# Routing four chunks of tokens at a time instead of two, in an attention and mixture-of-experts kernel

## The chip, the cores and the metric

The kernel runs on one NeuronCore of a Trainium2 chip. The metric is device time in microseconds (us) of one execution. The engines are named as in the profile: PE is TensorE (matmuls; PEld its weight loads), DVE is VectorE, ACT is ScalarE, POOL is GpSimd, SP is SyncE, which here only issues transfers.

## What is computed

```python
# attention without softmax, B, S, D = 8, 2496, 256, d_qk = 64
scores = matmul(z, z.T) / S
x = u * matmul(maximum(scores, 0) ** 2, v)            # 19968 rows of 256
# mixture of experts over the rows with x @ w_skip > 0, E = 8, F = 1024
logits = x @ w_gate;  e = argmax(logits)              # first of the largest
gate = softmax(logits)[e]
out = x + gate * (maximum(x @ w1[e], 0) @ w2[e])      # other rows: out = x
```

## The kernel before

**Precision.** Matmul operands are split into a high part (rounded to fp32r) and a low part (the rest): `zh, zl`, `vh, vl`, `ah, al`, `hh, hl`. A product is three matmuls: high by high, high by low, low by high. ACT (or DVE) rounds, DVE subtracts.

**Attention stage.** A chunk is 512 columns of queries (the fifth of each batch has 448); there are 8 x 5 = 40 chunks, and each has ten steps `p`, one for each pair of 128-row blocks of keys. `stage(s)` issues the scores of a step (`scores`, 6 matmuls with 64 rows each, into a PSUM tile of tag `"s"`, of which there are two), the ReLU and the square on ACT (lines 376, 377), the rounding to `ah` (386) and the low half `al` on DVE (390). `attend` issues 12 matmuls for each half of D (line 419). Scores run two steps ahead of `attend`. Where a score block was computed for an earlier chunk, its transpose is kept in DRAM (`keep`, DVE line 319) and read back (`recall`). At a chunk's end `finish` evacuates the accumulators (447 on ACT, 449 on DVE), multiplies by u in place (452: the u tile becomes the transposed x, `xT`) and turns it to rows (456) which SP stores.

The order on each engine is that of the program text (`tc.manual_schedule`). Work beside the steps is put off by hand: `todo[s]` holds functions that are called at the end of step `s`, `at(s, f)` counts in half steps, and `later` starts a load and calls its split some steps afterwards.

**Routing.** `routing(cis)` treats the chunks in `cis`, 4 tiles of 128 tokens each; `K = 4 * len(cis)`. Its parts are called at different steps:

- `gates`: 8 matmuls a chunk on PE in the program, 16 in the profile (line 491), with `wgs` as a 128x32 weight in one of four column strips, into a tile `psm` of tag `"s"`
- `logits`: DVE transposes `psm` to `lg` (514; a chunk of 448 columns needs separate transposes and a memset, 517, 518)
- `route`: DVE, six operations (525 to 534): the choice of expert, one-hot in `seq`
- `counts`: DVE, a scan over the tiles (543 to 552), which goes on from `run_cnt`, the count of the routing before
- `gate`: ACT, the exponential (555)
- `place`: four matmuls with 64 rows (564, weights `tri` and `ones`), a copy on ACT (570), seven DVE operations (572 to 579): each token's place in its expert's list
- `put_in(t, t + 2)`: DVE adds an offset (588), POOL puts two tiles' numbers and gates into `lst` in DRAM with two indirect transfers (590)

A routing is made up at the end of chunk 0, 2, 4 ... 38 and takes all chunks since the one before, so two, but one at the first. That of chunk 39 runs in the expert stage with 128-row matmuls.

**Expert stage.** From about 1245 us on, each expert takes units of 256 or up to 512 of its rows: POOL gathers x by `lst` (640), PE turns it (658) and runs the two layers (692, 711), POOL scatters the result (743). `load_w` brings the weights.

**Buffers that the change touches.** `ZBUFS = 7` buffers each for `zh` and `zl`; three u tiles; `rp` holds the routing's small tiles, two buffers of most. `"gap"` and `"gap2"` are tiles that nothing uses. At the start `f0` to `f3` round and split z's tiles 0 and 1 and v's tiles 0 and 1, all before the first scores. [...]

Of the kernel before, what the change touches and what calls it, by code (L numbers as in the profile page):

```python
# [11 lines left out]
I32 = mybir.dt.int32  # L12
# [28 lines left out]

C_REV, C_OFF, C_IDS, C_THR, C_TRI = 0, 64, 128, 132, 152

# [6 lines left out]
def attn_moe(ctx, tc, zT, uT, v, wg, w1, w2, cst, pad, out):  # L50
# [48 lines left out]

    ZBUFS = SZ // QC + 2  # L100

# [63 lines left out]
    def load_u(ci):  # L165
        b, q0, n = chunks[ci]
        uts[ci] = xp.tile([P, 2, QC], F32, name="ut", tag="ut", bufs=3)
        nc.sync.dma_start(uts[ci][:, :, :n], uT[b, :, :, q0 : q0 + n])
# [15 lines left out]
    load_u(0)  # L184
    for f in (f0, f1, f2, f3):
        f()
# [5 lines left out]
    wgs = cpool.tile([P, 2, 32], F32, name="wgs")  # L192
    cpool.tile([P, 88], F32, name="gap")
    nc.scalar.dma_start(wgs, wg)
# [3 lines left out]
    nc.gpsimd.tensor_copy(tri, trif)  # L198
    rev = cs[:, C_REV : C_REV + 64].rearrange("p (t e) -> p t e", e=E)
    eoff = cs[:, C_OFF : C_OFF + 64].rearrange("p (t e) -> p t e", e=E)  # L200
    ids0 = cs[:, C_IDS : C_IDS + 4]
    run_cnt = None
    goes_on = cpool.tile([P, E, 9], BF16, name="goes_on")
    nc.gpsimd.memset(goes_on, 1.0)
# [271 lines left out]
    def routing(cis, rows64=True):  # L476
# [3 lines left out]
        ins = [xTs.pop(ci) for ci in cis]  # L480
        lg = rp.tile([P, 8, 32], F32, name="lg", tag="lg")[:, :K, :]
        psg = []
# [12 lines left out]

        seq = rp.tile([P, E, 9], BF16, name="seq", tag="seq")
        pre = rp.tile([P, E, 9], BF16, name="pre", tag="pre")
        hot = seq[:, :, 1 : K + 1]
        pair = rp.tile([P, 8, 2], I32, name="pair", tag="pair", bufs=3)
        dest = rp.tile([P, 8], I32, name="dest", tag="dest", bufs=3)  # L500

        ex = rp.tile([P, 8, E], F32, name="ex", tag="ex")[:, :K, :]
        sm = rp.tile([P, 8, 1], F32, name="sm", tag="sm")[:, :K, :]

# [15 lines left out]
        def route():  # L520
            mx = rp.tile([P, 8, 1], F32, name="mx", tag="mx")[:, :K, :]
            dl = rp.tile([P, 8, E], F32, name="dl", tag="dl")[:, :K, :]
            rv = rp.tile([P, 8, E], F32, name="rv", tag="rv")[:, :K, :]
            rm = rp.tile([P, 8, 1], F32, name="rm", tag="rm")[:, :K, :]
            nc.vector.tensor_reduce(mx, lg[:, :, 0:E], axis=AX.X, op=ALU.max)
            dls.append(dl)
            nc.vector.tensor_sub(dl, lg[:, :, 0:E], mx.to_broadcast([P, K, E]))

            nc.vector.scalar_tensor_tensor(rv, dl, 0.0, rev[:, :K, :], op0=ALU.is_equal, op1=ALU.mult)
            nc.vector.tensor_reduce(rm, rv, axis=AX.X, op=ALU.max)  # L530
            nc.vector.scalar_tensor_tensor(
                rm, lg[:, :, E : E + 1], 0.0, rm, op0=ALU.is_gt, op1=ALU.mult
            )
            nc.vector.tensor_tensor(
                hot.rearrange("p e t -> p t e"), rev[:, :K, :], rm.to_broadcast([P, K, E]), op=ALU.is_equal
            )

        def counts():
            nonlocal run_cnt
            if run_cnt is None:  # L540
                nc.vector.memset(seq[:, :, :1], 0.0)
            else:
                nc.vector.tensor_copy(seq[:, :, 0], run_cnt)
            if K < 8:
                nc.vector.memset(seq[:, :, K + 1 :], 0.0)
            nc.vector.tensor_tensor_scan(
                *(x.rearrange("p e t -> p (e t)") for x in (pre, goes_on, seq)), 0.0, op0=ALU.mult, op1=ALU.add
            )
            run_cnt = pre[:, :, 8]
            for g, ci in enumerate(cis):  # L550
                b, q0, _ = chunks[ci]
                nc.vector.tensor_scalar_add(pair[:, 4 * g : 4 * g + 4, 0], ids0, float(b * S + q0))
# [4 lines left out]
        def place():  # L557
            ps = spare(rows64)
            ds_ = rp.tile([P, E, 8], F32, name="ds_", tag="ds_")[:, :, :K]
            df = rp.tile([P, 8], F32, name="df", tag="df")[:, :K]  # L560
            halves = list(enumerate(HALF)) if rows64 else [(0, slice(0, P))]
# [6 lines left out]

            c = rp.tile([P, 2, E * 8], F32, name="c", tag="c", bufs=1)[:, : len(halves), : K * E]
            nc.scalar.copy(c, ps[:, : len(halves), : K * E])  # L570
# [43 lines left out]
    idt_e = gp.tile([P, 2 * NFIX, 2], I32, name="idte")  # L614
    gp.tile([P, 32], F32, name="gap2")
    xgs = {"u": [], "f": []}
# [185 lines left out]
    for ci, (b, q0, n) in enumerate(chunks):  # L802
# [14 lines left out]
        if q0 == 0 and b + 1 < B:  # L817

            jobs = [(load_v, 0, 1, 3), (load_z, 0, 1, 6), (load_v, 1, 2, 3), (load_z, 1, 2, 5), (load_v, 2, 2, 7)]
            jobs += [(load_v, 3, 3, 3), (load_v, 4, 3, 4), (load_v, 5, 3, 6), (load_v, 6, 3, 7)]  # L820
            jobs += [(load_v, 7, 4, 2), (load_z, 2, 4, 3), (load_v, 8, 4, 4), (load_z, 3, 4, 5)]
            jobs += [(load_v, 9, 4, 6), (load_z, 4, 4, 7)]
            for load, j, c, k in jobs:
                later(s0 + c * NB + 2 * k - 7, 7, load, b + 1, j, nc.vector)
# [25 lines left out]
    for s in range(LA):  # L850
        for f in stage(s):
            f()
    accs = {}
    new, left = [], []
    for s, (ci, p) in enumerate(steps):
# [20 lines left out]
        else:  # L876
# [30 lines left out]
            if ci < NC - 1:  # L907
                after = [(rows0, 2), (rows1, 3), (store, 4), (store, 8)]
                if ci % 2 == 0:
                    gates, logits, route, counts, gate, place, put_in = routing(new)  # L910
                    after = [(gates, 2), (logits, 2), (rows0, 2), (rows1, 3), (route, 4), (counts, 4),
                             (store, 5 if ci == NC - 2 else 4), (gate, 5), (place, 6), (store, 8)]
                    for t in range(0, 4 * len(new), 2):
                        f = lambda put_in=put_in, t=t: put_in(t, t + 2)
                        if s + 6 + t < len(steps):
                            after.append((f, 6 + t))
                        else:
                            left.append(f)
# [22 lines left out]
    def end_counts():  # L941
# [11 lines left out]

        late = rp.tile([P, 8, 1], F32, name="late", tag="sm")[:, 0, :]
        nc.vector.tensor_scalar(
# [18 lines left out]
    def turned(e, i):  # L974
        if e and i == 0:
            if not xtf:
                for _ in range(2):
                    t = xp.tile([P, 2 * QC], F32R, name="xtf", tag="ut", bufs=3)
                    xtf.append(t[:, 80 : 80 + QC].rearrange("p (d q) -> p d q", d=2))
            return xtf  # L980
# [147 lines left out]
```

## Time and profile before

| | us |
|---|---|
| median of three runs | 1725.46 |
| lowest, highest | 1724.9, 1727.47 |
| the profiled execution | 1724.65 |
| its span, first to last instruction | 1722.7 |

The granted clock of TensorE was 0.999 of full speed over the span. In the rows below times are in us from the span's start, unless they are marked ns or stand as a mean; a row of a timeline has start, length, engine, line, operation, what is written and read, and how many instructions were merged into it (`x4`). A bracket at its end tells how long the engine had been idle, and who ended that. A length of a matmul is modelled and longer than the time to the next one's start.

### The profile page before, as it was taken

The numbers are of one execution on the slowest core, as the hardware profiler recorded it, in microseconds if no ns is written. First come the engines' busy times: TensorE is split into PE (matmuls) and PEld (weight loads), VectorE is DVE, ScalarE is ACT, GpSimd is POOL, SyncE is SP. The second block draws the span as 40 slices with busy tenths as digits, with TensorE's granted clock in tenths as the row PEclk, the third lists the DMA queues.
The fourth block names the chain that finished last, engine by engine and source line by source line (L and its number), as shares of the span: only waits on it lengthen the run. The fifth ranks groups of instructions, "written<-read, shape, count | busy, mean of one in ns | idle before, by whom it ended". The sixth has DMA issues, their size and how long they took to land.

```text
span 1722.7 us, 39254 instructions
## 1 busy us (share of the span) xinstructions
PE 1710.2 (99%) x15474; PEld 1522.8 (88%) x15474; DVE 1199.4 (70%) x1969; ACT 1118.9 (65%) x1416; POOL 519.6 (30%) x516
## 2 busy tenths in 40 slices
PE   9999999999999999999999999999999999999998
PEld 7888889988888898888889988888999999999997
DVE  7877877887887888778888778777754334344433
ACT  8877877787687778768777886877433333333321
POOL 1103203212311320231132132122355556645731
PEclk9999999999999999999999999999999999999999
DMA  5586699589868958985895799578752333323210
GB/s 191 144 212 188 154 248 285 144 209 263 246 148 235 260 165 203 273 265 135 226 250 178 197 259 276 134 216 223 212 130 76 88 95 107 91 63 97 87 43 27
DMA packets 408108, 303.25 MB, mean 176 GB/s; under 512 B 202768, under 2 KB 346001, under 8 KB 407152
## 3 DMA queue, kind: packets, MB, share of 16 engines
q1 hardware_dynamic: 393728, 276.37, 59.0%
q0 software_dynamic: 13632, 22.99, 4.7%
q8 instruction: 137, 2.24, 0.5%
q14 instruction: 179, 1.47, 0.3%
q10 hardware_dynamic: 432, 0.18, 0.0%
HBM read 184.21 MB, written 136.02 MB: 186 GB/s over the span
## 4 chain that ended last, share of the span: by engine, by line
PE 93%; DMA 3%; issue 2%; ACT 1%; DVE 1%; POOL 0%; SPq 0%; POOLq 0%; ACTq 0%; DVEq 0%
PE acc L419 59%; PE y L711 12%; PE psh L692 11%; PE ps L302 9%; DMA out<-o,idt 2%; PE psm L491 1%; PE pst L658 1%; PE ps L285 0%; DMA out<-xr 0%; DVE al L390 0%; DMA raw<-in_v 0%; ACT r L377 0%; ACT ah L386 0%; ACT r L376 0%; DVE rt L319 0%
## 5 line engine op out<-in xcount | busy, mean ns | idle before, releaser
L419 PE MATMUL acc<-ah,vh 64*128 64x512 f32 (+1 forms) x3120 | 639.6, 383 | 0.8 <-DVE ah L386 0.8
L419 PE MATMUL acc<-ah,vl 64*128 64x512 f32 (+1 forms) x3120 | 625.5, 382 | 0.0
L390 DVE TENSOR_TENSOR al<-r,ah 128x1024 fp32r<-128x1024 f32 (+1 forms) x400 | 479.0, 1205 | 134.7 <-ACT ah L386 128.3
L419 PE MATMUL acc<-al,vh 64*128 64x512 f32 (+1 forms) x3120 | 496.4, 383 | 0.4 <-DVE al L390 0.2
L590 POOL DMA_INDIRECT lst<-pair,dest x160 | 202.0, 1262 | 765.9 <-DVE dest L588 735.8
L386 ACT CAST ah<-r 128x1024 fp32r<-128x1024 f32 (+1 forms) x363 | 370.0, 1030 | 82.3 <-PE acc L419 46.9
L419 PEld LDWEIGHTS acc<-ah,vh 64*128 64x128 f32 x3120 | 325.8, 184 | 49.3 <-issue 1.4
L419 PEld LDWEIGHTS acc<-ah,vl 64*128 64x128 f32 x3120 | 326.0, 184 | 43.6 <-DVE vl L122 0.3
L419 PEld LDWEIGHTS acc<-al,vh 64*128 64x128 f32 x3120 | 309.8, 184 | 51.0 <-DVE al L390 6.3
L376 ACT ACTIVATE r<-ps 128x1024 f32<-128x1024 f32 (+1 forms) x224 | 227.9, 1018 | 132.5 <-PE ps L302 123.8
L697 ACT ACTIVATE hh<-psh 128x512 fp32r<-128x512 f32 (+2 forms) x172 | 96.4, 571 | 269.4 <-PE psh L692 254.2
L377 ACT ACTIVATE r<-r 128x1024 f32<-128x1024 f32 (+1 forms) x224 | 235.9, 1053 | 7.1
L711 PE MATMUL y<-w2t,hh 128*128 128x256 f32 (+1 forms) x1328 | 235.2, 280 | 0.0
L698 DVE SCALAR_TENSOR_TENSOR hl<-psh,hh 128x512 fp32r<-128x512 f32 (+2 forms) x172 | 110.2, 655 | 138.6 <-ACT hh L697 131.5
L319 DVE STREAM_TRANSPOSE rt<-r 128x512 f32<-128x512 f32 x304 | 197.4, 687 | 9.4 <-DMA kept<-rt 8.6
L711 PEld LDWEIGHTS y<-w2t,hh 128*128 128x128 f32 (+1 forms) x1328 | 200.6, 185 | 1.2
L711 PE MATMUL y<-w2t,hl 128*128 128x256 f32 (+1 forms) x664 | 184.2, 277 | 0.0
L692 PE MATMUL psh<-xt,w1h 128*128 128x256 f32 (+3 forms) x896 | 181.1, 300 | 1.9 <-DVE hl L698 1.9
L692 PEld LDWEIGHTS psh<-xt,w1h 128*128 128x128 f32 x896 | 140.4, 188 | 7.2 <-DVE hl L698 3.2
L692 PE MATMUL psh<-xt,w1l 128*128 128x256 f32 (+3 forms) x448 | 133.8, 299 | 0.0
L743 POOL DMA_INDIRECT out<-o,idt x77 | 76.4, 992 | 159.3 <-DVE o L740 126.4
L711 PEld LDWEIGHTS y<-w2t,hl 128*128 128x128 f32 (+1 forms) x664 | 122.6, 185 | 0.0
(197 smaller groups left out, 1735.4 us busy)
## 6 DMA issues: line engine op xcount, KB each, us to landing
kept<-rt SPq DMA_DIRECT2D x242, 256.0 KB, 4.9
r<-kept SPq DMA_DIRECT2D x90, 512.0 KB, 6.0
r<-kept SPq DMA_DIRECT2D x62, 448.0 KB, 7.2
raw<-in_v SPq DMA_DIRECT2D x80, 256.0 KB, 5.8
ut<-in_uT SPq DMA_DIRECT2D x32, 512.0 KB, 6.2
xr<-xrow SPq DMA_DIRECT2D x128, 128.0 KB, 3.7
out<-xr SPq DMA_DIRECT2D x32, 512.0 KB, 6.4
raw<-in_w SPq DMA_DIRECT2D x64, 256.0 KB, 4.0
```

The costliest lines, as they stand in the source:

```text
L302: nc.tensor.matmul(to, k[h, o : o + P], queries(ci, q, h, n), start=(m == 0), stop=(m == 2))
L319: nc.vector.transpose(t[:, :, 32 * k : 32 * k + 32].rearrange("p (k a) i -> p a k i", k=4), r[:, x, :].rearrange("p (a k i) -> p a k i", a ...
L376: nc.scalar.activation(r[:, :, :n], ps[:, :, :n], AF.Relu, scale=isc)
L377: nc.scalar.activation(r[:, :, :n], r[:, :, :n], AF.Square)
L386: (nc.scalar.copy if on_act(ci, p) else nc.vector.tensor_copy)(h_, r_)
L390: nc.vector.tensor_sub(l_, r_, f32(h_))
L419: nc.tensor.matmul(acc[t][:, :n], w[h, x, dd], a[h, x, :n], start=(first and t not in halves[:m]), stop=(last and t not in halves[m + 1 :]),)
L590: put = nc.gpsimd.indirect_dma_start(out=lst, out_offset=bass.IndirectOffsetOnAxis(ap=dest[:, t : t + 1], axis=0), in_=pair[:, t, :], in_o ...
L692: nc.tensor.matmul(ps[:, j * W : (j + 1) * W], wt[:, a, o : o + P], x[:, d, :W], start=(m == 0), stop=(m == 5),)
L697: nc.scalar.activation(hh[:, : G * W], ps[:, : G * W], AF.Relu)
L698: nc.vector.scalar_tensor_tensor(hl[:, : G * W], ps[:, : G * W], 0.0, f32(hh[:, : G * W]), op0=ALU.max, op1=ALU.subtract)
L711: nc.tensor.matmul(ys[t], h[:, tt], w2t[f][:, k, :], start=(f == 0 and m == 0 and t % share == 0), stop=(f == NF - 1 and m == 2), skip_gro ...
```

## The change

1. A routing is made up after chunks 0, 4, 8 ... 36 and after 38 (of the last two). Tiles for up to `KG = 16` token tiles; to find the room most of them have one buffer, and `c` shares a buffer with `lg`. With four chunks `counts` is called at step 5 behind the chunk's end (4 before), `place` at 7 (6), and the eight pairs of puts at 7, 8, 10, 11, 13, 14, 16, 17 (four at 6, 8, 10, 12).
2. Five u tiles in place of three, `ZBUFS` 6 in place of 7; the load of z's tile 1 for batch 1 moves from chunk 2 to chunk 4 of batch 0.
3. `f3`, the split of v's tile 1, is called after the first step's `stage`.
4. The scratch for indirect transfers is 8192 bytes.

```diff
+KG = 16
-C_REV, C_OFF, C_IDS, C_THR, C_TRI = 0, 64, 128, 132, 152
+C_REV, C_OFF, C_IDS, C_THR, C_TRI = 0, 128, 256, 260, 280
-    ZBUFS = SZ // QC + 2
+    ZBUFS = SZ // QC + 1
-        uts[ci] = xp.tile([P, 2, QC], F32, name="ut", tag="ut", bufs=3)
+        uts[ci] = xp.tile([P, 2, QC], F32, name="ut", tag="ut", bufs=5)
-    for f in (f0, f1, f2, f3):
+    for f in (f0, f1, f2):
         f()
-    cpool.tile([P, 88], F32, name="gap")
+    cpool.tile([P, 440], F32, name="gap")
-        lg = rp.tile([P, 8, 32], F32, name="lg", tag="lg")[:, :K, :]
+        lg = rp.tile([P, KG, 32], F32, name="lg", tag="lg", bufs=1)[:, :K, :]
...
-            c = rp.tile([P, 2, E * 8], F32, name="c", tag="c", bufs=1)[:, : len(halves), : K * E]
+            c = rp.tile([P, 2, E * KG], F32, name="c", tag="lg", bufs=1)[:, : len(halves), : K * E]
-    gp.tile([P, 32], F32, name="gap2")
+    gp.tile([P, 408], F32, name="gap2")
-            jobs = [(load_v, 0, 1, 3), (load_z, 0, 1, 6), (load_v, 1, 2, 3), (load_z, 1, 2, 5), (load_v, 2, 2, 7)]
+            jobs = [(load_v, 0, 1, 3), (load_z, 0, 1, 6), (load_v, 1, 2, 3), (load_v, 2, 2, 7)]
+            jobs += [(load_z, 1, 2, 5) if b else (load_z, 1, 4, 6)]
     for s in range(LA):
         for f in stage(s):
             f()
+        if s == 0:
+            f3()
-                if ci % 2 == 0:
+                if ci % 4 == 0 or ci == NC - 2:
                     gates, logits, route, counts, gate, place, put_in = routing(new)
-                    after = [(gates, 2), (logits, 2), (rows0, 2), (rows1, 3), (route, 4), (counts, 4),
-                             (store, 5 if ci == NC - 2 else 4), (gate, 5), (place, 6), (store, 8)]
+                    many = len(new) > 2
+                    after = [(gates, 2), (logits, 2), (rows0, 2), (rows1, 3), (route, 4), (counts, 5 if many else 4),
+                             (store, 5 if ci == NC - 2 else 4), (gate, 5), (place, 7 if many else 6), (store, 8)]
                     for t in range(0, 4 * len(new), 2):
                         f = lambda put_in=put_in, t=t: put_in(t, t + 2)
-                        if s + 6 + t < len(steps):
-                            after.append((f, 6 + t))
+                        k = 6 + (1 + 3 * t // 4 if many else t)
+                        if s + k < len(steps):
+                            after.append((f, k))
-    nc = bacc.Bacc("TRN2", target_bir_lowering=False, num_devices=1)
+    nc = bacc.Bacc("TRN2", target_bir_lowering=False, num_devices=1, dynamic_dma_scratch_size=8192)
```

The other lines of the diff write `KG` for 8, `KG + 1` for 9 and `KG * E` for 64 in the routing's tiles and constants.

## Rows read from the trace of the kernel before

**Rows 1.** The profile's page: busy time of the engines (share of the span, instructions), and the shares of the chain of work that ended last, by engine.

```profile
PE 1710.2 (99%) x15474; PEld 1522.8 (88%) x15474; DVE 1199.4 (70%) x1969; ACT 1118.9 (65%) x1416; POOL 519.6 (30%) x516
PE 93%; DMA 3%; issue 2%; ACT 1%; DVE 1%; POOL 0%; SPq 0%; POOLq 0%; ACTq 0%; DVEq 0%
```

**Rows 2.** The waits of PE's matmuls, first and last of five rows: engine and line that waited, for whom; us in total, times, longest.

```profile
PE psh L692 <- DVE hl L698: 1.9, 3, 1.1
...
PE acc L419 <- DVE al L390: 0.2, 1, 0.2
```

**Rows 3.** The longest wait of PE's weight loads, same columns.

```profile
PEld acc L419 <- DVE al L390: 6.3, 18, 0.6
```

**Rows 4.** One piece of the chain in order of time, in undisturbed attention: start, us, what, how many.

```profile
118.46 5.45 PE acc L419 x48
```

**Rows 5.** PE's timeline around the gates of two chunks.

```profile
174.86 0.61 PE L419 MATMUL acc<-al,vh 64*128 64x512 f32 x4
175.40 1.07 PE L491 MATMUL psm<-ut,wgs 128*32 128x128 f32 x32
176.41 0.50 PE L302 MATMUL ps<-zqh,zh 64*128 64x512 f32 x2
176.75 0.40 PE L302 MATMUL ps<-zql,zh 64*128 64x512 f32 x2
```

**Rows 6.** PE's timeline around the gates of one chunk (chunk 0).

```profile
50.24 0.61 PE L419 MATMUL acc<-al,vh 64*128 64x512 f32 x4
50.78 0.65 PE L491 MATMUL psm<-ut,wgs 128*32 128x128 f32 x16
...
51.70 0.40 PE L302 MATMUL ps<-zql,zh 64*128 64x512 f32 x2
```

**Rows 7.** PE's timeline around the placing of one chunk (first two rows) and of two chunks.

```profile
64.68 0.61 PE L419 MATMUL acc<-al,vh 64*128 64x512 f32 x4
...
65.51 0.39 PE L302 MATMUL ps<-zql,zh 64*128 64x512 f32 x2
...
129.42 0.61 PE L419 MATMUL acc<-al,vh 64*128 64x512 f32 x4
129.88 0.21 PE L564 MATMUL psm<-seq,tri 64*128 64x64 bf16 x2
...
130.26 0.39 PE L419 MATMUL acc<-ah,vl 64*128 64x512 f32 x2
```

**Rows 8.** The instructions that write or read `psm`, over the whole span: duration in ns (least, median, most), first and last start, forms.

```profile
L570 ACT COPY c<-psm x21: 185/257/265, 65.7 to 1252.7; 128x128 f32<-128x128 f32 x19, 128x64 f32<-128x64 f32 x1, 128x32 f32<-128x32 f32 x1
```

**Rows 9.** The start: rows of ACT's timeline, and PE's first two groups of `al` matmuls.

```profile
6.73 0.62 ACT L121 CAST vh<-raw 128x512 fp32r<-128x512 f32 x1
7.26 1.02 ACT L376 ACTIVATE r<-ps 128x1024 f32<-128x1024 f32 x1
9.27 1.00 ACT L376 ACTIVATE r<-ps 128x1024 f32<-128x1024 f32 x1
11.41 0.73 PE L419 MATMUL acc<-al,vh 64*128 64x512 f32 x4
13.61 0.62 PE L419 MATMUL acc<-al,vh 64*128 64x512 f32 x4
```

**Rows 10.** The one-hot, DVE's longest routing operation, by shape, with 64 elements (two chunks) and 32 (one chunk): busy us, mean ns of one, idle time before.

```profile
L534 DVE TENSOR_TENSOR seq<-cs,rm 128x64 bf16<-128x64 f32 x19 | 8.6, 452 | 0.6
L534 DVE TENSOR_TENSOR seq<-cs,rm 128x32 bf16<-128x32 f32 x2 | 0.6, 304 | 0.1
```

**Rows 11.** DVE's timeline in chunk 7: first and last of `route` (6 rows), last of `counts` (4 rows), first of `place` and the first put's (8 rows).

```profile
251.15 0.18 DVE L525 TENSOR_REDUCE mx<-lg 128x8 f32<-128x64 f32 x1
...
252.34 0.45 DVE L534 TENSOR_TENSOR seq<-cs,rm 128x64 bf16<-128x64 f32 x1
...
253.41 0.17 DVE L552 TENSOR_SCALAR pair<-cs 128x4 int32<-128x4 f32 x1 [0.20 <-issue]
...
257.62 0.18 DVE L572 TENSOR_REDUCE sm<-ex 128x8 f32<-128x64 f32 x1
...
259.26 0.17 DVE L588 TENSOR_SCALAR dest<-df 128x2 int32<-128x2 f32 x1
```

**Rows 12.** The transposes behind the gates of rows 5 (DVE's timeline, first and last), and the scores that next use their PSUM buffer (PE's).

```profile
178.79 0.47 DVE L514 STREAM_TRANSPOSE lg<-psm 128x128 f32<-128x128 f32 x2
179.43 0.26 DVE L518 STREAM_TRANSPOSE lg<-psm 32x64 f32<-32x64 f32 x1
179.94 0.39 PE L302 MATMUL ps<-zqh,zh 64*128 64x512 f32 x2
```

**Rows 13.** POOL's longest wait; an indirect gather behind another; and the indirect transfers of the expert stage and the puts by line, with the median us from issue to landing.

```profile
POOL lst L590 <- DVE dest L588: 735.8, 65, 52.8
1268.08 1.00 POOL L640 DMA_INDIRECT xgu<-xr,go  x1 [0.30 <-DVE o L740]
lst<-pair,dest POOLq DMA_INDIRECT x160, 5.9
out<-o,idt POOLq DMA_INDIRECT x77, 2.8
xgf<-xr,go POOLq DMA_INDIRECT x48, 3.3
xgu<-xr,go POOLq DMA_INDIRECT x48, 2.9
```

More of the change, by code (lines that the diff above doesn't have):

```diff
@@ L198, in attn_moe @@
     nc.gpsimd.tensor_copy(tri, trif)
-    rev = cs[:, C_REV : C_REV + 64].rearrange("p (t e) -> p t e", e=E)
-    eoff = cs[:, C_OFF : C_OFF + 64].rearrange("p (t e) -> p t e", e=E)
+    rev = cs[:, C_REV : C_REV + KG * E].rearrange("p (t e) -> p t e", e=E)
+    eoff = cs[:, C_OFF : C_OFF + KG * E].rearrange("p (t e) -> p t e", e=E)
     ids0 = cs[:, C_IDS : C_IDS + 4]
     run_cnt = None
-    goes_on = cpool.tile([P, E, 9], BF16, name="goes_on")
+    goes_on = cpool.tile([P, E, KG + 1], BF16, name="goes_on")
     nc.gpsimd.memset(goes_on, 1.0)
@@ L494, in gates @@
                         )
-        seq = rp.tile([P, E, 9], BF16, name="seq", tag="seq")
-        pre = rp.tile([P, E, 9], BF16, name="pre", tag="pre")
+        seq = rp.tile([P, E, KG + 1], BF16, name="seq", tag="seq")
+        pre = rp.tile([P, E, KG + 1], BF16, name="pre", tag="pre")
         hot = seq[:, :, 1 : K + 1]
[L499 to L503, printed above, removed]
+        pair = rp.tile([P, KG, 2], I32, name="pair", tag="pair", bufs=3)
+        dest = rp.tile([P, KG], I32, name="dest", tag="dest", bufs=3)
+        ex = rp.tile([P, KG, E], F32, name="ex", tag="ex", bufs=1)[:, :K, :]
+        sm = rp.tile([P, KG, 1], F32, name="sm", tag="sm")[:, :K, :]
         def logits():
@@ L520, in route @@
         def route():
[L521 to L524, printed above, removed]
+            mx = rp.tile([P, KG, 1], F32, name="mx", tag="mx")[:, :K, :]
+            dl = rp.tile([P, KG, E], F32, name="dl", tag="dl", bufs=1)[:, :K, :]
+            rv = rp.tile([P, KG, E], F32, name="rv", tag="rv", bufs=1)[:, :K, :]
+            rm = rp.tile([P, KG, 1], F32, name="rm", tag="rm")[:, :K, :]
             nc.vector.tensor_reduce(mx, lg[:, :, 0:E], axis=AX.X, op=ALU.max)
@@ L543, in counts @@
                 nc.vector.tensor_copy(seq[:, :, 0], run_cnt)
-            if K < 8:
+            if K < KG:
                 nc.vector.memset(seq[:, :, K + 1 :], 0.0)
@@ L548, in counts @@
             )
-            run_cnt = pre[:, :, 8]
+            run_cnt = pre[:, :, KG]
             for g, ci in enumerate(cis):
@@ L558, in place @@
             ps = spare(rows64)
-            ds_ = rp.tile([P, E, 8], F32, name="ds_", tag="ds_")[:, :, :K]
-            df = rp.tile([P, 8], F32, name="df", tag="df")[:, :K]
+            ds_ = rp.tile([P, E, KG], F32, name="ds_", tag="ds_", bufs=1)[:, :, :K]
+            df = rp.tile([P, KG], F32, name="df", tag="df")[:, :K]
             halves = list(enumerate(HALF)) if rows64 else [(0, slice(0, P))]
@@ L952, in end_counts @@
         nc.vector.tensor_reduce(nmore, more, axis=AX.X, op=ALU.add)
-        late = rp.tile([P, 8, 1], F32, name="late", tag="sm")[:, 0, :]
+        late = rp.tile([P, KG, 1], F32, name="late", tag="sm")[:, 0, :]
         nc.vector.tensor_scalar(
@@ L977, in turned @@
                 for _ in range(2):
-                    t = xp.tile([P, 2 * QC], F32R, name="xtf", tag="ut", bufs=3)
+                    t = xp.tile([P, 2 * QC], F32R, name="xtf", tag="ut", bufs=5)
                     xtf.append(t[:, 80 : 80 + QC].rearrange("p (d q) -> p d q", d=2))
@@ L1104 @@
     cst[:, C_TRI : C_TRI + P] = np.triu(np.ones((P, P)), 1)
-    cst[:, C_REV : C_REV + 64] = np.tile(E - np.arange(E), 8)
-    cst[:, C_OFF : C_OFF + 64] = np.tile(np.arange(E) * CAP - BIG, 8)
+    cst[:, C_REV : C_REV + KG * E] = np.tile(E - np.arange(E), KG)
+    cst[:, C_OFF : C_OFF + KG * E] = np.tile(np.arange(E) * CAP - BIG, KG)
     tok = np.arange(4 * P).reshape(4, 4, 32).transpose(0, 2, 1).reshape(P, 4)
```

## The prediction

> **What bounds the kernel now.** I read the page first [rows 1]: the multiplying engine (PE) is busy for 1710.2 of 1722.7 us and is 93% of the chain that ended last. The list of waits [rows 2] says the same from the other side: PE's matmuls stood idle for a named engine in five kinds of wait, from 1.9 us down to 0.2 us, so 9.5 us at the very most. Its weight loads waited for the vector engine's (DVE's) low halves 18 times, 6.3 us, at most 0.6 us at once [rows 3]. So until about 1245 us the time is the length of PE's own queue, and a change there gains what it takes out of that queue. It gains nothing by making DVE, ACT or POOL lighter.
>
> The busy digits can't show what the queue loses between two kinds of matmul, because a matmul's modelled length (0.39 us for a pair) is longer than its pitch. The timeline's starts show it. The undisturbed pitch is 48 matmuls in 5.45 us [rows 4], 0.227 us for a pair that runs in the two 64-row halves.
>
> **The gates.** In [rows 5] a block of 32 gate matmuls (two chunks) stands between attention pairs. The four `al` matmuls before it start at 174.86; two pairs later, at 175.31, the next thing could start, and a second pair after it at 175.54. With the block in between, the second pair starts at 176.75: the block costs 1.21 us. In [rows 6] the block of one chunk has 16 matmuls: three pairs on from 50.24 is 50.92, the second pair starts at 51.70, cost 0.78 us. So 16 matmuls more cost 0.43 us, and what is left, 0.78 - 0.43 = 0.35 us, is paid per block whatever is in it. It is seen as 0.09 us before the first gate matmul and 0.34 instead of 0.23 us between the first two pairs behind it; the rest is the end of the block.
>
> Placing does the same on a smaller scale [rows 7]: 129.42 + 0.68 = 130.10, second pair at 130.26, 0.16 us with 64 columns for each matmul; with 32 columns, 64.68 + 0.68 = 65.36 against 65.51, 0.15 us.
>
> **How many blocks go.** There are 40 chunks. Before, a routing closes after chunks 0, 2, 4 ... 38, and one for the last chunk runs in the expert stage: 21, which the 21 copies of `c` confirm (19 with 8 tiles, 2 with 4) [rows 8]. After, it closes after chunk 0, after 4, 8 ... 36 (nine of four chunks), after 38 (two chunks), and the last: 12. Nine blocks of each kind go. The number of gate matmuls (640) stays.
>
> - Gates: 9 x 0.35 = 3.15 us. Reading a start to 0.01 us at three places leaves 2.8 to 3.4.
> - Placing: before, 19 x 0.16 + 0.15 = 3.2 us. After, 0.15 + 0.16 + 9 blocks with 128 columns, a form that the trace does not show. From below it costs what 64 columns cost, 0.16. From above, its two pairs of 128 columns each take as long as a whole 512-column pair does for a quarter of its columns (0.057) on top of a block: 0.16 + 0.11 = 0.27. With 32 columns it was 0.15, so doubling them cost 0.01; from 64 to 128 the columns should begin to count, and I take 0.22, the middle. That is 2.3, a saving of 0.9 us (0.5 to 1.45).
>
> **The start.** `f3` rounds and splits v's second tile before the first activation. In [rows 9] ACT's copy starts at 6.73 and the first ReLU follows it at 7.26. With `f3` behind step 0 the ReLU takes the copy's place, so the first `ah` and `al`, and PE's first `al` matmul at 11.41, come 0.53 us earlier, up to 0.7 if the copy itself had waited for its tile. But the copy now stands before the ReLU of step 1, which then stays near 9.27, and the split stands on DVE between the first `al` and the second `ah`. PE meets its next condition at 13.61, the second `al`, which follows step 1's ReLU and so can come hardly sooner than before; what PE gains there is what it had waited behind other matmuls. Bounds are 0 and 0.7; I take 0.25 us.
>
> **What is moved and hidden.** DVE's small operations become fewer and longer. From 32 to 64 elements the choice's costliest grows by half, 0.304 to 0.452 us [rows 10]. If from 64 to 128 all grew by half, `route` (251.15 to 252.8, 1.65 us) [rows 11] would be 2.5 us; it is a burst of 2.5 us now with `counts` (to 253.6), which goes to the next step, so neither burst exceeds the old one. `place`, now one step later, is 1.8 us (257.62 to 259.4); its bounds are 1.8 and 2.7, and I take 2.2, since its operations are the short ones. All this is hidden while PE's step (30 matmuls with scores, 3.4 us by the pitch in [rows 4], 24 without, 2.7) is longer than DVE's work; if it isn't, the next `al` is late (first rival). The logits of four chunks are up to six transposes in place of four, which hold a score buffer longer. In [rows 12] they run 178.79 to 179.69 and that buffer's next scores start at 179.94, a margin of 0.25 us. After, PE comes 0.86 us later (32 more gate matmuls) and DVE ends 0.47 us later (two transposes more at 0.235, the pitch there): margin 0.64 us, no wait. [...]
>
> The 16 indirect puts go to steps 7 to 17 in pairs; POOL stood idle 735.8 us before puts [rows 13], and the chunk's `straight` copies stand ahead of the puts of their step. The u tiles' fourth and fifth buffers keep four chunks' x until their gates; the slot that a load takes is that of five chunks before, whose gates ran a half chunk earlier, so SP's loads wait for nothing new. One z buffer fewer moves one z load of batch 1 to chunk 4 of batch 0, where it adds a copy on ACT (0.62 us for such a tile in [rows 9]) and a split on DVE: nothing to the path while the step has room, some 0.6 us once if it has none.
>
> **Sum.** 3.15 + 0.9 + 0.25 = 4.3 us off. The profiled execution took 1724.65 (span 1722.7), so 1720.35; the median of the runs, 1725.46, is 0.8 above it and would come to 1721.15. I forecast 1720.7, between the two. About 0.2%, 3.45 us, is what a measurement here can tell from no change; from the median that is 1722.0.
>
> **Rivals.**
> 1. *DVE gives it back.* Place: `place` one step nearer the chunk's end, where DVE also evacuates accumulators. [Rows 11] show the risk: from 251.15 to 259.4 DVE pauses once, for 0.20 us. Price: 0.4 us longer plus the 0.1 us that PE loses when it restarts (0.34 instead of 0.23 us behind the gates in [rows 5]), in nine routings: 4.5 us. With the 4.3 gained that is 1725.6, no change. For it: the full stretch. Against: nine other bursts vanish, and all 21 and everything else cost at most 6.3 us together [rows 3]. Half of it, 1723, is no change too. Chance 0.25.
> 2. *The saving is swallowed later*, at the chunk ends where `al` is late anyway: then only blocks far from one count, say half, 2.2 us, 1723.2. Against: PE has next to no idle time to swallow it. Chance 0.07.
> 3. *Slower: the halved scratch.* Each indirect transfer of the expert stage is issued 1.3 us after the one before and lands about 3 us after its issue [rows 13], so two or three are under way. If the halved scratch holds only one, POOL waits out each landing: the stage's 173 gathers and stores would take 173 x 3 = 519 us in a stage of 478 (from 1245 to the end), and x for the matmuls would come late: some 40 us and more, 1765. It decides once fewer than three fit. Nothing in the trace says how many the old size held beyond what was under way, some four puts (5.9 us to land, two of them a step). Chance 0.04. [...]
> Small delays of several kinds that together exceed 8 us: 0.04, also slower.
>
> **Numbers.** Forecast 0.60 for a gain of about 4.3 us; its own range, with the terms' bounds and runs that differ by 2.5 us, is 1718.5 to 1722. Faster by over 0.2%: 0.60. Within: rivals 1 and 2, 0.32. Slower: 0.08. For 8 in 10 the range goes from 1718 up to the end of rival 1: 1718 to 1726.
>
> **What would show it.** Twelve copies of `c`; blocks of 64 gate matmuls that cost about 2.07 us by the reading above, and placing blocks near 0.22. PE's first `al` matmul near 10.9 instead of 11.41, with a wait before the second. The row of weight loads waiting for `al` at or under 6.3 us: if it is over 10, rival 1 holds. If POOL's indirect rows are longer than 1.3 us apart where they stand back to back, rival 3 holds. The forecast is wrong if the fixed 0.35 us grows with the block, or if moved tiles change the pitch of 0.227 us.

## The result and the profile after

On one chip the changed kernel took 1738.6 us against 1726.8 us (medians): ratio 1.0064, 95% interval 1.0049 to 1.0078. These are its fast runs; a sixth, slow one took 8890 us and is not counted. It is 11.8 us slower, where 4.3 us faster was forecast, and lies outside the range of 1718 to 1726. The profiled execution took 1738.62 us (span 1736.5) against 1724.65 (span 1722.7).

| us | attention ends (start of PE's last `acc` matmul) | from there to PE's last matmul | from there to the end |
|---|---|---|---|
| before | 1242.5 | 473.3 | 7.0 |
| after | 1247.1 | 480.1 | 9.3 |

Between the two profiled executions the loss has three places: +4.6 us in attention, where the gain of 4.3 was due, +6.8 in the expert stage, whose program is unchanged, and +2.3 behind PE's last matmul. Lines of after are one higher than before's from the start to the middle of the program.

The page (busy; shares of the chain) answers [rows 1]: PE's share falls from 93 to 81%, and DMA's rises from 3 to 7%.

```profile
PE 1714.8 (99%) x15438; PEld 1531.7 (88%) x15438; DVE 1183.0 (68%) x1840; ACT 1117.3 (64%) x1398; POOL 518.8 (30%) x516
PE 81%; DMA 7%; DVE 3%; issue 3%; ACT 2%; POOL 1%; SPq 1%; POOLq 0%; DVEq 0%; ACTq 0%
```

The waits of PE's weight loads answer [rows 3] (waiter, for whom: us in total, times, longest). `al` is late 34 times instead of 18, and `ah`, which ACT rounds, is late 8 times.

```profile
PEld acc L420 <- DVE al L391: 13.4, 34, 0.7
PEld acc L420 <- ACT ah L387: 5.8, 8, 2.2
```

PE's timeline, first at the start and then around the first gates of four chunks, answers [rows 9] and [rows 5].

```profile
10.83 0.73 PE L420 MATMUL acc<-al,vh 64*128 64x512 f32 x4
...
13.35 0.73 PE L420 MATMUL acc<-al,vh 64*128 64x512 f32 x4
...
173.21 0.61 PE L420 MATMUL acc<-al,vh 64*128 64x512 f32 x4
173.76 1.95 PE L492 MATMUL psm<-ut,wgs 128*32 128x128 f32 x64
175.63 0.50 PE L303 MATMUL ps<-zqh,zh 64*128 64x512 f32 x2
175.97 0.40 PE L303 MATMUL ps<-zql,zh 64*128 64x512 f32 x2
...
192.31 0.61 PE L420 MATMUL acc<-al,vh 64*128 64x512 f32 x4
...
193.19 0.39 PE L303 MATMUL ps<-zql,zh 64*128 64x512 f32 x2
```

The first `al` matmul is at 10.83 (10.9 forecast). The block of 64 gate matmuls costs 175.97 - 173.21 - 0.68 = 2.08 us (2.07 forecast), placing with 128 columns 193.19 - 192.31 - 0.68 = 0.20 (0.22 forecast). `c` is copied 12 times. So the gain is there, as computed; other things take it away. Three are seen at once in the profile.

**Late scores.** The chain of waits between 229 and 239 us, where PE loses 1.9 us, and what PE then waits for:

```profile
229.22 7.30 DMA r<-kept
...
236.62 1.05 ACT ah L387
237.71 0.51 PE L420 MATMUL acc<-ah,vh 64*128 64x512 f32 x2 [1.76 <-ACT ah L387]
```

The same recall in the kernel before, SP's issue and the `ah` that follows its landing:

```profile
228.31 1.44 SPq L359 DMA_DIRECT2D r<-kept  x1
234.61 1.05 ACT L386 CAST ah<-r 128x1024 fp32r<-128x1024 f32 x1 [0.58 <-DMA r<-kept]
```

Recalled scores land 7.3 us after their issue, and `ah` starts only then. In before the issue is 0.9 us sooner and `ah` starts 6.3 us behind it, not 7.4. Sixteen puts run from 197 to 231 us, in before eight from 197 to 216. At 850 us, twenty chunks on, the same happens (a recall that lands 7.6 us after its issue).

**The last branch.** PE's timeline at the last expert's branch, and the windows behind it (length, PE, PEld, DVE, ACT, POOL busy, granted clock, DMA share, GB/s; in brackets instructions). The last two rows of the first list are the kernel before's:

```profile
1627.16 0.60 PE L659 MATMUL pst<-ident,xgf 128*128 128x128 f32 x4
1630.17 0.66 PE L693 MATMUL psh<-xt,w1h 128*128 128x256 f32 x2 [2.42 <-issue]
1620.03 0.60 PE L658 MATMUL pst<-ident,xgf 128*128 128x128 f32 x4
1620.38 0.48 PE L692 MATMUL psh<-xt,w1h 128*128 128x256 f32 x2
```

```profile
1627.00:1630.20 3.20, 0.79 (x8) 0.58 (x6) 1.48 (x3) 0.58 (x1) 3.04 (x5) 1.00 0.35 72
1630.20:1634.00 3.80, 3.80 (x19) 3.80 (x20) 0.15 (x1) 0.60 (x1) 2.88 (x4) 0.55 0.32 82
1634.00:1639.00 5.00, 5.00 (x45) 5.00 (x44) 2.61 (x5) 2.27 (x4) 0.79 (x1) 1.00 0.15 54
```

PE waits for nothing that the profile shows ("issue"): 3.0 us from one row to the next, 0.35 in before. Behind the pause the granted clock is 0.55 on the mean of the stretch, and 19 matmuls run in its 3.8 us where the later rate (45 in 5.00 us) gives 34; the 15 missing cost 1.7 us. Together 4.4 us.

**The end.** From the start of POOL's last transfer to the end of the span it is 1736.5 - 1728.33 = 8.2 us, in before 1722.7 - 1716.82 = 5.9.

### The profile page after: what moved, and what is told of

Same layout as the page of the kernel before. It is cut to its first block, busy times and chain, and to the rows that moved or that the text cites. A ratio compares the mean times of both kernels' runs of the same rounds, so it can differ in the third digit from the quotient of the medians.

```text
span 1736.5 us, 39038 instructions
## 1 busy us (share of the span) xinstructions
PE 1714.8 (99%) x15438; PEld 1531.7 (88%) x15438; DVE 1183.0 (68%) x1840; ACT 1117.3 (64%) x1398; POOL 518.8 (30%) x516
## 4 chain that ended last, share of the span: by engine, by line
PE 81%; DMA 7%; DVE 3%; issue 3%; ACT 2%; POOL 1%; SPq 1%; POOLq 0%; DVEq 0%; ACTq 0%
PE acc L420 52%; PE y L712 10%; PE psh L693 9%; PE ps L303 8%; DMA r<-kept 3%; DMA out<-o,idt 2%; DVE al L391 2%; DMA xgf<-xr,go 1%; PE psm L492 1%; ACT ah L387 1%; PE pst L659 1%; ACT r L377 1%; ACT r L378 1%; SPq L470 0%; PE ps L286 0%
## 5 line engine op out<-in xcount | busy, mean ns | idle before, releaser
L420 PE MATMUL acc<-ah,vh 64*128 64x512 f32 (+1 forms) x3120 | 648.3, 383 | 3.6 <-ACT ah L387 3.3
L420 PE MATMUL acc<-ah,vl 64*128 64x512 f32 (+1 forms) x3120 | 635.4, 382 | 0.0
L420 PE MATMUL acc<-al,vh 64*128 64x512 f32 (+1 forms) x3120 | 505.2, 384 | 1.3 <-DVE al L391 0.5
L420 PEld LDWEIGHTS acc<-ah,vh 64*128 64x128 f32 x3120 | 338.1, 184 | 51.8 <-ACT ah L387 5.8
L420 PEld LDWEIGHTS acc<-ah,vl 64*128 64x128 f32 x3120 | 337.8, 184 | 41.7 <-DVE vl L123 0.3
L420 PEld LDWEIGHTS acc<-al,vh 64*128 64x128 f32 x3120 | 315.7, 184 | 55.0 <-DVE al L391 13.4
L264 POOL CAST zqh<-zh 128x512 fp32r<-128x512 f32 (+2 forms) x47 | 36.6, 790 | 494.1 <-PE ps L286 209.2
```

The lines of the kernel that those rows point to most:

```text
L420: nc.tensor.matmul(acc[t][:, :n], w[h, x, dd], a[h, x, :n], start=(first and t not in halves[:m]), stop=(last and t not in halves[m + 1 :]),)
```

## The experiments

The experiments ran on several chips; on some the kernel before took 1726 to 1727 us and on others 1736 to 1737, so ratios are to its runs beside them. "Pause" is that of the last branch, from PE's transposes of `xgf` to the next matmul; "end" is from the start of POOL's last transfer (the expectations count it from that transfer's end, 1.0 us less). The ratios come from all counted runs, the other three columns from one profiled execution each, so differences of a microsecond or two between rows of different chips say little. One chip ran `x0_after`, `e7_sparse`, `e5_early` and `e6_noputs`; one `e1_two` to `e4_dense`; one `x1_before`, `e9_light`, `e10_b12k` and `e11_bnoputs`; one the other six.

| kernel | ratio to before (95%) | attention ends | pause | end |
|---|---|---|---|---|
| before, twice (`x1_before`) | | 1242.5, 1242.9 | 0.35, 0.35 | 5.9, 5.8 |
| after | 1.0064 (1.0049 to 1.0078) | 1247.1 | 3.0 | 8.2 |
| `x0_after` | 1.0064 (1.0046 to 1.0082) | 1251.9 | 3.0 | 8.2 |
| `e1_two` | 1.0018 (1.0004 to 1.0031) | 1242.7 | 0.35 | 7.9 |
| `e2_scratch` | 1.0016 (1.0004 to 1.0027) | 1243.5 | 0.35 | 8.0 |
| `e3_f3` | 0.9993 (0.9981 to 1.0004) | 1243.0 | 0.35 | 5.8 |
| `e4_dense` | 1.0336 (1.0294 to 1.0378) | 1294.2 | 3.7 | 8.0 |
| `e7_sparse` | 1.0072 (1.0046 to 1.0098) | 1245.0 | 3.2 | 8.0 |
| `e5_early` | 1.0066 (1.0048 to 1.0084) | 1247.8 | 3.1 | 7.9 |
| `e6_noputs` | not compared | 1242.3 | 3.2 | |
| `e11_bnoputs` | not compared | 1244.3 | 0.35 | |
| `e15_pace` | 1.0056 (1.0038 to 1.0073) | 1243.1 | 3.4 | 7.9 |
| `e9_light` | 1.0024 (1.0013 to 1.0034) | 1240.5 | 3.2 | 7.9 |
| `e12_pad` | 1.0047 (1.0029 to 1.0065) | 1244.9 | 0.35 | 8.1 |
| `e14_bpad` | one run | 1244.1 | 2.4 | 5.8 |
| `e10_b12k` | 1.0004 (0.9992 to 1.0016) | 1243.5 | 0.35 | 6.3 |
| `e13_all` | 1.0079 (1.0058 to 1.0100) | 1246.6 | 0.35 | 5.8 |
| `e16_apart` | 1.0019 (1.0002 to 1.0035) | 1241.8 | 0.35 | 8.0 |
| `e17_room` | 1.0022 (1.0004 to 1.0039) | 1244.9 | 0.35 | 6.0 |

### Which part of the change

```diff
# e1_two (to after)
-                if ci % 4 == 0 or ci == NC - 2:
+                if ci % 2 == 0 or ci == NC - 2:
# e2_scratch (to before)
-num_devices=1)
+num_devices=1, dynamic_dma_scratch_size=8192)
# e3_f3 (to before): only f3 moved, as in the change
```

> The changed kernel with its routing made up after every second chunk, as before, with the old steps for counts, place and puts; the tiles, the five u tiles, the six z buffers, the moved z load, f3 behind the first step and the halved scratch stay as changed. It tells the size of a routing apart from the memory around it. Theory P (the puts and the longer routing are late and lie beside transfers of the chunk after next): the 12 us of loss are gone and the time is that of before, 1726, less 0.3 for the start. Theory D (DVE's bursts, one step later): the same, 1726; P and D are told apart by other runs. Theory M (the halved scratch, the fewer z buffers or moved addresses): the loss stays, 1736 or more, since the gain of fewer blocks (4 us) is given up and nothing of the loss is. Theory C (the expert stage and the end lose time by where the program's instructions lie, or by chance): about 1731, with the end of attention near 1242 as before and about 5 us lost behind it.

> The kernel before with the halved scratch for indirect transfers alone. Theory M says slower by several us, in the expert stage above all, where the changed kernel lost about 7 us behind the end of attention (at most 1733). Theories P, D and C say no change: 1726, with attention's end near 1242.5 and the expert stage as long as before, 480 us.

> The kernel before with f3, the split of v's second tile, called behind the first step's stage and nothing else. In the trace of the changed kernel PE's lag behind the kernel before was -0.26 us after the start. All theories: 0.26 us less than before (1726.5), which a time can hardly show; the profile's first al matmul and the start of the second step should show it. If the rest of the program shifts by more than 1 us in either direction, something in it hangs on the phase of the start.

Routing two chunks with all the rest of the change ends attention where before did and has no pause. So both go with the routing of four, and the z and u buffers and moved loads cost nothing that shows there. The scratch alone (8192 bytes in place of before's 16384) costs as much as all of `e1_two`, some 3 us by the ratios, of which 2.1 are at the end. `f3` alone can't be told from no change.

### The puts

```diff
# e4_dense (to after): k = 7, 7, 8, 8, 9, 9, 10, 10
-                        k = 6 + (1 + 3 * t // 4 if many else t)
+                        k = 6 + (1 + t // 4 if many else t)
# e7_sparse: k = 7, 11, ... 35;  e15_pace: k = 7, 9, ... 21 (both up to chunk 32's routing)
+                        k = 6 + (1 + (2 * t if ci < NC - 4 else 3 * t // 4) if many else t)
+                        k = 6 + (1 + (t if ci < NC - 4 else 3 * t // 4) if many else t)
# e5_early: counts at 4, place at 6, as before
# e6_noputs, e11_bnoputs: in put_in
+                if K == KG:                             # e6_noputs, to after
+                    continue
+                if K == 8 and cis[-1] < NC - 4:         # e11_bnoputs, to before
+                    continue
```

> The changed kernel with its puts drawn together: four at each of the steps 7 to 10 behind a routing's close, so that they end inside the next chunk, in place of two at each of the steps 7, 8, 10, 11, 13, 14, 16, 17. Theory P: the losses that were seen beside late puts (236, 850 us: 2 us each; 573 and 1187, 1.3 us each) go, and the end of attention comes 4 us or more sooner than the 1247.1 of the changed kernel, 1243 or less; if bunched puts only move the crowding, new stalls appear inside the next chunk. Theory D: no change at the end of attention, 1247 (DVE's place and counts stand where they were). Theory M: no change.

I had taken a long run of puts for the harm, and closer puts for a remedy. The kernel is 62 us slower than the one before, and attention 47 us longer than in the changed kernel. The waits of PE's weight loads, and the windows around one run of puts (445 to 470 us):

```profile
PEld acc L420 <- issue: 41.9, 66, 1.4
```

```profile
450.00:455.00 5.00, 5.00 (x50) 4.31 (x46) 3.19 (x6) 2.69 (x4) 3.99 (x4) 1.00 0.94 308
455.00:460.00 5.00, 4.67 (x37) 3.11 (x33) 3.06 (x5) 1.11 (x2) 3.88 (x4) 1.00 0.94 248
460.00:465.00 5.00, 3.96 (x24) 2.25 (x25) 2.12 (x3) 2.32 (x3) 3.97 (x4) 1.00 0.93 158
465.00:470.00 5.00, 3.76 (x14) 1.70 (x13) 1.91 (x3) 0.08 (x1) 3.89 (x4) 0.73 1.03 256
470.00:475.00 5.00, 4.32 (x21) 3.99 (x23) 2.20 (x3) 2.82 (x4) 1.55 (x3) 0.50 0.72 157
```

PE slows from 50 matmuls in 5 us to 14, and then the clock falls too, to 0.73 and 0.50. It waits for nothing that the profile shows; that it starves for its own instructions is the reading that I take, and not shown. The trace has packets of 16384 bytes on an instruction queue of their own (`q8`, 136 in the changed kernel), which I take for PE's; between 444 and 480 us they come 16.9 and 19.3 us apart. That alone proves nothing: in before two come 18.1 us apart (437.72, 455.79) while PE stays busy.

> The changed kernel once more, beside the three others of this call, since the kernel before has moved from 1726 to 1736 us between the first comparison and the second. All theories: its ratio to the kernel before stays near 1.0064, with attention's end near 1247 and the rest of the loss in the expert stage. If the loss behind attention is chance or the place of the program's instructions, the expert stage is now no longer than that of the other kernels.

> The changed kernel with its pairs of puts thinned out: one pair every fourth step (7, 11, 15 ... 35 behind the close) for the routings of chunks 4 to 32, in place of eight pairs within eleven steps. [...] Theory P: attention ends near 1239 to 1241 (before 1242.5, changed 1247.1), the predicted 4 us are there, and the time is some 6 us under the changed kernel. Theory D (place and counts are late on DVE): attention still ends near 1247.

> The changed kernel with counts at step 4 and place at step 6 behind the close, as before, and the puts where the change has them. Theory D: the waits for al (13.4 us on PE's weight loads) fall towards 6 and attention ends 3 us or more sooner than 1247. Theory P: no change there, or worse, since route and counts then stand in one burst: 1247 to 1249.

> The changed kernel without the indirect puts of its nine routings of four chunks; their tokens' numbers are missing from the lists, so the experts gather padding rows for them and only the attention stage is to be read. Theory P: attention ends at the predicted place or sooner, 1238 us, and the recalled scores (r from kept) land on time at 236 and 850 us. Theory D: the stalls at 236, 573, 850 and 1187 us stay and attention ends near 1247.

`x0_after` repeats the ratio and the pause, but attention ends 4.8 us later than in the first profile of the same kernel, and its expert stage, 485.0 us, is about as long as that of `e1_two` (484.5) and `e2_scratch` (485.9), on another chip of the slower kind. So the 6.8 us that the expert stage lost in the first pair of profiles are not seen there.

Thinner puts end attention 6.9 us sooner than `x0_after` on the same chip, and no puts 9.5 us. In `e7_sparse` 2.4 us of what is left are one place (596 us), where a pair of puts stands ahead of the `zqh` copies on POOL. Its time didn't follow: its four runs differed by 9 us, and the profiled one was the quickest. The row of `al` waits in `e6_noputs` is 11.4 us, so DVE's part stays without puts. `e5_early` is a miss for DVE as I had put it: the waits stay at 11.4 us, against 12.3 in `x0_after`. Its attention ends 4.1 us sooner than `x0_after`'s, but gains this at 239, 482 and 851 us, where `e6_noputs` gains too.

On this chip a part of the puts' price is again waits of PE's weight loads for nothing that is seen, in attention 6.6 us in `x0_after` and 1.2 in `e6_noputs` (0.6 in the first profile of the changed kernel):

```profile
PEld acc L420 <- issue: 6.6, 13, 1.2
PEld acc L420 <- issue: 1.2, 6, 0.2
```

What else the puts do is seen in one window, 220 to 235 us, of `x0_after`, then `e6_noputs` (same chip), then `x1_before`; the last two rows are the first profiles of after and before:

```profile
220.00:235.00 15.00, 14.56 (x132) 11.76 (x132) 9.04 (x13) 12.28 (x14) 8.39 (x10) 1.00 0.86 186
```

```profile
220.00:235.00 15.00, 15.00 (x138) 12.39 (x136) 10.18 (x13) 12.56 (x15) 2.17 (x2) 1.00 0.88 214
```

```profile
220.00:235.00 15.00, 15.00 (x138) 12.46 (x136) 10.56 (x12) 13.68 (x16) 2.17 (x2) 1.00 0.93 236
```

```profile
220.00:235.00 15.00, 15.00 (x138) 12.39 (x136) 9.47 (x13) 11.86 (x14) 8.05 (x10) 1.00 0.83 176
220.00:235.00 15.00, 15.00 (x138) 12.43 (x136) 10.55 (x12) 13.00 (x15) 2.16 (x2) 1.00 0.93 215
```

With puts in it the same stretch moves 176 and 186 GB/s, without 214, 215 and 236. The recall that PE waits for is issued at 229.58 us with puts and at 227.92 without (same chip), and `ah` starts 7.5 us behind it instead of 6.4. That the puts crowd the DMA engines is my reading of this; these rows don't show where on the way the time goes.

> The kernel before without the indirect puts of its routings of two chunks up to chunk 34; their tokens' numbers are missing from the lists, so only the attention stage is to be read. It prices the puts at the old pace (one pair every second step). If every put costs something wherever it stands, attention ends several us before 1243, as the changed kernel's did without puts (1242.3 for 1247 to 1252). If only the closer pace costs, it ends within 1 us of 1243.

> The changed kernel with its puts at the old pace, a pair every second step (7, 9, 11 ... 21 behind the close) for the routings of chunks 4 to 32; all else as changed. The kernel before lost nothing in attention by its puts at that pace (e11_bnoputs). If only the closer pace costs, attention ends within 1 us of where it did without puts, 1242.3; if 16 puts in a row cost at any pace, it ends at 1245 or later.

At the old pace puts are free: before's attention is no shorter without them (1244.3, of which 1.2 came at its start), and four chunks' puts at that pace end it at 1243.1, 0.8 us from no puts (on another chip). The price of the closer pace is not one number: 9.5 us on the chip of `x0_after`, but 1.8 on that of `e15_pace`, where `e12_pad`, with 37 matmuls more at its start, keeps the closer pace and ends attention at 1244.9.

### The bursts on DVE

`e6_noputs` ends attention 4.1 us behind the 1238.2 that the forecast's sum gives. The largest slips are at 446, 570, 692, 1059 and 1183 us, some seven steps behind a routing. DVE there, in `e6_noputs`, with the PE row that waits for it, and in the kernel before:

```profile
438.40 2.36 DVE L391 TENSOR_TENSOR al<-r,ah 128x1024 fp32r<-128x1024 f32 x2
440.67 0.28 DVE L573 TENSOR_REDUCE sm<-ex 128x16 f32<-128x128 f32 x1
...
442.76 0.38 DVE L580 TENSOR_REDUCE df<-ds__6240 128x16 f32<-128x128 f32 x1
...
443.87 1.22 DVE L391 TENSOR_TENSOR al<-r,ah 128x1024 fp32r<-128x1024 f32 x1
445.14 0.73 PE L420 MATMUL acc<-al,vh 64*128 64x512 f32 x4 [0.47 <-DVE al L391]
```

```profile
440.77 0.21 DVE L572 TENSOR_REDUCE sm<-ex 128x8 f32<-128x64 f32 x1
...
442.15 0.28 DVE L579 TENSOR_REDUCE df<-ds__6448 128x8 f32<-128x64 f32 x1
...
442.57 1.23 DVE L390 TENSOR_TENSOR al<-r,ah 128x1024 fp32r<-128x1024 f32 x1
...
444.31 1.22 DVE L390 TENSOR_TENSOR al<-r,ah 128x1024 fp32r<-128x1024 f32 x1
```

DVE has no pause from 429 to 445 us in either: keeping scores and splitting v fill it. `place` takes 2.5 us instead of 1.7, and since it is called a step later, the `al` behind it is that of the next step. In before this `al` stands at 444.31, now at 443.87, only 0.4 us sooner though PE is 1.9 us ahead; PE waits for it. So:

```diff
# e9_light (to after); counts, gate and place likewise
+                    w = {2: 10, 1: 20, 0: 30}.get(ci % NQ, 0) if many and ci < NC - 4 else 0
-(route, 4)
+(route, w + 4)
+                        k = 6 + (w + 1 + t if many and ci < NC - 4 else ...)
```

> The changed kernel with choice, counts, places and puts of a routing put off by 10, 20 or 30 steps where they would fall into the second to fourth chunk of a batch, so that they run in a fifth or first chunk (gates stay where they are; the routing of chunk 36 is not put off); the puts are one pair every second step, the pace of the kernel before. Theory: the loss in attention has two parts, DVE's longer bursts where DVE has no pause (4 to 5 us, what is left without puts) and puts too close together beside recalls and instruction fetches (5 to 9 us). Both should go but for the routing of chunk 36 (about 1.6 us): attention ends near 1240, and the time, with 2.1 us of the scratch at the end, is about that of before. If attention ends above 1244, the two parts do not explain the loss.

Attention ends at 1240.5, as expected, 2.4 us under `x1_before` on the same chip. This shows that burst and pace together hold most of attention's loss. The burst's part can be told apart by place: against `e6_noputs`, which has no puts but the bursts, `e9_light` gains 0.7 to 1.4 us at 446, 570 and 1059 us and 0.5 at 692, the places whose bursts it moves. The slip at 1183 us, behind chunk 36, whose routing it doesn't put off, stays (1.1 us). `e15_pace`, with the same pace and the bursts in place, still has the one at 570 (1.3 us).

### The last branch and the end

```diff
# e12_pad (to after); e14_bpad (to before) with 92
+    for _ in range(37):
+        nc.tensor.matmul(psw[:32, 0, :1], ones[:, :32], ones[:, :1], start=True, stop=True)
```

> The changed kernel with 37 more matmuls of one column at the start, behind the 50 that warm PE up. It has 36 matmuls fewer than the kernel before, and all eight kernels so far that route four chunks at once had PE wait 2.4 to 3.1 us for instructions at the last expert's branch, 106 us before their end, and none of the seven that route two. Theory L (where the instructions lie): with the number restored that wait is gone, and the half-rate matmuls behind it (1.6 us) too: the expert stage is some 4 us shorter than the changed kernel's 480 and, since the start comes 0.5 to 1.5 us later, the time is about 3 us under it (ratio to before near 1.0047). Theory S (the smaller scratch or the routing itself delays the last branch): the wait stays.

> The kernel before with 92 more matmuls of one column at the start, 184 instructions with their weight loads. [...] Theory L: the wait for instructions at the last expert's branch, 106 us before the end, appears in this kernel too, 2 to 3 us. Theory S: it doesn't. The start is 3 to 5 us later by either.

With 37 matmuls more at the start, 1.6 ms earlier, the pause is gone, in all four kernels that have them; all eight traces of the table that route four chunks without them have it. The profile names nothing that PE waits for there; that these are waits for instructions, as the expectations say, is a reading. The ratio fell to the expected 1.0047; its interval overlaps that of `x0_after`, so the pause is the proof and not the time. Shifting the kernel before gives it a pause (the number 92 was an estimate of mine; no run shows how far it moves the instructions):

```profile
1631.64 0.60 PE L660 MATMUL pst<-ident,xgf 128*128 128x128 f32 x4
1634.01 0.47 PE L694 MATMUL psh<-xt,w1h 128*128 128x256 f32 x2 [1.76 <-ACT xtf L662]
```

The wait is put down to ACT's `xtf`, but this matmul reads `xt`, and in before it started 0.35 us behind the transposes that `xtf` is copied from. That 2.4 us lie here is measured; that PE lacks its instructions here too is a reading. For it speaks when the instruction packets start: in this kernel at 1631.13 and 1634.54, in the changed one at 1627.53, just as PE runs dry, and 1630.64, but in before at 1614.38 and 1619.72, both ahead of the branch at 1620, and in `e12_pad` at 1630.05, 5.4 us ahead of it.

> e3_f3 with a scratch of 12288 bytes in place of 16384. From the last transfer of POOL to the end of the span it took 4.9 and 4.8 us with 16384 bytes, 7.0 us with 8192. If the size itself sets this, it is between, 5.5 to 6.5 us. [...] The rest is as in e3_f3.

6.3 us with 12288 bytes, 5.3 counted as in the expectation and so under its 5.5 to 6.5; in `e13_all` 5.8 with 10240, where 16384 gave 5.8 and 8192 gave 7.9 to 8.2. It isn't a matter of size alone. In the trace POOL's last drain is 1.87 us with 16384 bytes, 2.20 with 12288, 1.88 with 10240 and 3.59 with 8192. In `e11_bnoputs`, with 16384 bytes but fewer transfers issued before, it is 8.00 us. So at one size it differs between kernels; what sets it is not shown.

### All together

```diff
# e13_all = e9_light + e12_pad + scratch 10240, without the tiles "gap" and "gap2"
# e16_apart = e9_light + e12_pad, and chunk 24's puts six steps later
# e17_room = e16_apart + scratch 10240, without "gap" and "gap2"
+                        k = 6 + (w + 1 + t + 6 * (ci == 24) if many and ci < NC - 4 else ...)
```

> The kernel before, for a profile on the chip on which the experiments ran, since its profile of step one is some 10 us shorter than its times there. With e3_f3 as the nearest kernel so far, attention should end near 1243 and the expert stage take near 483 us (473 in the first profile), with waits of PE for its own instructions; then the part of the changed kernel's loss behind attention that is not in its last 9 us is no effect of the change.

> All remedies together: e9_light (late parts of the routing put off to a first or fifth chunk, puts at the old pace), the 37 matmuls of e12_pad, and a scratch of 10240 bytes, with the two unused tiles taken out to make room for it. Attention should end near 1241 (1240.5 in e9_light, a later start by up to 1), the expert stage take as long as that of the kernel before, and the end be 0 to 2 us longer: 1 to 3 us under before, ratio 0.998 to 0.9995. If the account of the loss is incomplete it stays above before.

> e9_light with the 37 matmuls of e12_pad and the puts of chunk 24's routing six steps later, so that they no longer fall among those of chunk 20's, which e9_light had put off by 30 steps; the scratch is the halved one. In e13_all the one large stall of attention (some 5 us near 816 us, ah late) lay where these two runs of puts met. If that was its cause it is gone: attention ends between 1239 and 1241, the wait at the last branch is absent, the end keeps its 2.1 us of the halved scratch, and the time is within 0.1% of before, on the faster side. If a stall of over 2 us stays near 810 us, its cause is another.

> The same with the scratch of 10240 bytes, for which the two unused tiles are taken out. The end was 4.8 us from POOL's last transfer in e13_all, as with 16384 bytes. Expected 2 us under e16_apart, 0.1 to 0.2% under before. If it is slower than e16_apart, moving the tiles costs more than the end gives back, and e13_all's loss was not of the puts alone.

`x1_before` was on a chip of the quick kind (1725.5), its expert stage 473.9 and not near 483; so those 10 us go with the chip, though no profile of the kernel before on a slower chip was taken. `e13_all` lost 5 us at 816 us, where puts of two routings met. With them apart a slip of 1.1 us stays there. But in `e9_light` they meet as well, and it loses only 1.6 us there, with DVE's `place` in the chain; so the meeting alone isn't shown to be the cause of the 5 us. `e16_apart` and `e17_room` are 0.2% above before: what they have left in attention (1 us for `e16_apart`) doesn't pay for the end or, in `e17_room`, for new waits for `ah` (5.9 us against 2.5). Whether those come from its moved tiles wasn't settled; its profiled execution was also the longest of its twelve. No version that routes four chunks beat the kernel before.

## Why the prediction was wrong

- *Gates, placing, start*: right in mechanism and size: 2.08 for 2.07, 0.20 for 0.22; PE is 0.26 us ahead behind the start (0.25 forecast).
- *DVE hidden*: this step failed. Its sizes held (`route` 2.2 us for 2.5, `place` 2.5 for 2.2). The condition, that PE's step is longer than DVE's work, was read at one chunk [rows 11], where DVE paused once, and not in those where it never does. It cost about 4.1 us (`e6_noputs` against the forecast's 1238.2), near rival 1's price (4.5), and rival 1's test, a row of `al` over 10 us, came true (13.4).
- *The 16 puts*: this step failed most. They were costed on POOL's idle time alone [rows 13] and so put at nothing. Pairs on two of three steps instead of every second made recalls late, and in two of four profiles PE waited another 5.1 and 6.6 us for nothing that is seen: 9.5 us between `x0_after` and `e6_noputs` on one chip, 4.8 if the first profile (1247.1) is set against the same 1242.3 from another chip. That the DMA engines are the place is argued, not shown; at 596 us of `e7_sparse` it was POOL's queue after all.
- *The scratch*: rival 3 did not occur (in the expert stage POOL's indirect transfers stay 1.3 us apart where they stand back to back, as in before). But the end was not in the sum: 2.2 us.
- *The number of PE's instructions*: not thought of. With 36 matmuls fewer, a branch that the diff doesn't touch paused: 4.4 us in the first profile.

Together: -4.3 + 4.1 + 4.8 + 4.4 + 2.2 = 11.2 us. These terms are read from profiled executions, whose spans differ by 13.8 us; that the sum is near the 11.8 between the medians is luck. The 4.1 and 4.8 are the two halves of 1247.1 - 1238.2, so they must add up to attention's loss and don't test it. The rest of the expert stage, 6.8 - 4.4 = 2.4 us, and the spread between chips are not explained.

## What to carry to other kernels

Read the cover for work that is made coarser in the fullest stretch that it will land in, not in one that is at hand. Cost a small transfer by the other transfers under way at that moment, not only by the engine that issues it, and keep its pace when its number is doubled. When PE's instruction count changes ahead of a branch, look at that branch in the new profile before looking for an engine to blame.

## What the runs showed of the hardware

- With indirect puts of 128 rows back to back (1.3 to 2.0 us apart) PE's weight loads waited 41.9 us for nothing that the profile shows (`e4_dense`); with pairs on two of three steps 0.6 to 6.6 in four profiles; with a pair every second step 0.8 to 2.1, and 1.2 without puts (`e6_noputs`).
- PE's pause at the last branch came and went (0.35 or 2.4 to 3.7 us) with 36 to 92 matmuls fewer or more ahead of it, and in the changed kernel the granted clock was 0.55 on the mean of the 3.8 us behind it.
- POOL's last drain took 1.87, 2.20, 1.88 and 3.59 us with 16384, 12288, 10240 and 8192 bytes of scratch, so with no order by its size, and 8.00 with 16384 and fewer transfers before it (`e11_bnoputs`).
